# Squared-ReLU attention and feed-forward in one kernel: last keys transposed on their own, the centering mean from one sum, one batch's score bursts moved by a column

## Chip, cores, metric

One core of a Trainium2 chip. The metric is the device time of one execution in microseconds (us). The chip gives several executions of each kernel.

## The reference, cut to what matters

```python
# batch 8, heads 12, seq S = 448, head_dim 64, d_model 768, d_ff 3072
scores = scale * np.matmul(q, k.transpose(0, 1, 3, 2))
attn = np.maximum(scores, 0.0) ** 2 / S
x = np.matmul(attn, v)                       # then heads side by side: (8, 448, 768)
mu = np.mean(x, axis=-1, keepdims=True)
var = np.mean((x - mu) ** 2, axis=-1, keepdims=True)
xn = (x - mu) / np.sqrt(var + 1e-06) * g_ln
out = x + np.maximum(xn @ w_ch1, 0.0) @ w_ch2
```

## The kernel before

The order of work is written by hand. The first batch's attention runs alone (about 29 us). From then on the attention of batch b+1 is fed in "bursts" between the 24 columns of the first feed-forward layer of batch b. A column is 12 half-width matmuls and takes 1.13 us. A burst is three score tiles: TensorE makes scores, ScalarE and VectorE apply the ReLU, VectorE squares. Two heads make a pair; there are 48 pairs, six for each batch. The attn-V product of a pair ("attn-V" below) is put on TensorE at the start of a later burst. From the third batch on, q and k are transposed by DMA (`dma_start_transpose` on the SyncE queue); earlier ones by TensorE.

```python
def load_early():                       # first two heads: staged as fp32, cast on chip
    ...
    nc.sync.dma_start(k_st[:SS, :, NF], k[0, :2, SF:].rearrange("h s d -> s h d"))   # last 64 keys
    nc.vector.tensor_copy(first_q[0][:, :2], q_st.rearrange("p (h j d) -> p h j d", h=2, j=NJ))
    nc.scalar.copy(first_k[0][:, :2, :NF], k_st[:, :, :NF])
    nc.vector.tensor_copy(first_k[0][:SS, :2, NF], k_st[:SS, :, NF])
...
def av_out(i, ps, evac_by):             # eviction of attn-V, then what the centering needs
    ...
    if b == 0:
        if pr < GAIN_FIRST:             # GAIN_FIRST = 3: "gain multiplication"
            nc.vector.tensor_scalar(xc[:, pr, :], xT_of(b, pr), g_sb[:, pr:pr + 1], None, op0=Alu.mult)
    elif pr == 1:
        nc.vector.tensor_add(xs, xT_of(b, 0), xT_of(b, 1))
    elif 1 < pr < NPAIR - 1:            # running sum of the first five parts
        nc.vector.tensor_add(xs, xs, xT_of(b, pr))
...
def first():                            # the mean: ones times (sum of five), plus ones times the sixth
    for n, part in enumerate((xs, xT_of(b, K1 - 1))):
        for c in range(2):
            nc.tensor.matmul(mean_ps[c * D:(c + 1) * D, :], ones[:, :D], part,
                             start=(n == 0), stop=(n == 1))
...
def excursion(n, ...):                  # a burst
    if len(ready) > 1: ...              # attn-V of two pairs together
    elif ready and ready[0] % NPAIR == NPAIR - 2:
        next_AV(**how)                  # attn-V of pair 16 (batch 2), at batch 1's seventh burst
    took = [slots.pop(0) for _ in range(n)]
    for m, (i, t) in enumerate(took):
        att_QK(i, t, ...)
    for i, t in took:
        att_square(i, t)
...
STATS_AT = {0: (18, 21, 23), 1: (10, 16, 19, 22), 2: (2, 5, 8, 14)}
IN_REST = (1, 4, 7, 10, 13, 16, 19)
...
bursts = IN_FIRST if b == 0 else [n + (2 if b == 1 else 0) for n in IN_REST]   # b == 1: 3,6,9,12,15,18,21
```

## Time and profile before

| | before |
|---|---|
| executions | 521.97 (median), 521.89, 522.72 us |
| profiled execution | 522.75 us, span 521.0 us |
| TensorE busy | 513.3 us, 99% |
| first matmul of the feed-forward ("first weight matmul") | 29.03 us |

From part 1 of the page of before: engine, busy time (share of the span), instructions.

```profile
PE 513.3 (99%) x5705; PEld 311.5 (60%) x5705; DVE 367.6 (71%) x650; ACT 277.1 (53%) x456; POOL 222.5 (43%) x255
```

From the waits view of before, TensorE only: who waited for what, total us, times, longest. TensorE's only wait after the start-up:

```profile
PE sc L284 <- DMA qkT_t<-qk_ring: 1.0, 1, 1.0
```

From the timeline of before, batch 1's first layer. Columns: start, duration, engine, line, operation, out and in, count, and in brackets idle time before it and what ended it. SPq is the SyncE queue issuing DMAs; `qkT_t` is a transposed q/k tile, `at` an attention tile, `xc` the centred activations.

```profile
96.98 4.93 SPq L256 DMA_TRANSPOSE qkT_t<-qk_ring  x2
...
102.53 0.35 PE L284 MATMUL sc<-qkT_t 64*64 64x448 bf16 x2
...
103.87 0.38 PE L284 MATMUL sc<-qkT_t 64*64 64x448 bf16 x2 [0.99 <-DMA qkT_t<-qk_ring]
...
115.10 3.57 PE L429 MATMUL f<-xc,w 128*64 128x448 bf16 x36
...
116.82 1.69 DVE L302 TENSOR_TENSOR at<-at 128x896 bf16<-128x896 bf16 x3
...
118.51 0.92 PE L319 MATMUL f<-at,v_ring 128*64 128x448 bf16 x8
...
119.36 0.55 PE L289 MATMUL sc<-qkT_t 64*128 64x448 bf16 x4
```

Read it in two halves. The second half of the fourth burst's last-key scores (103.87 us) waits 0.99 us for a transpose that was issued at 96.98 us. Further down, the 36 matmuls after the sixth burst are three columns; VectorE's three squarings of that burst end at 116.82 + 1.69 = 118.51 us; the attn-V of pair 16 (8 matmuls, `at` as input) starts at the same time and the seventh burst's scores at 119.36 us.

From the chain that ended last, before (start, us, engine and line, count), at a mean:

```profile
196.07 0.38 PE f L388 x4
```

The four mean matmuls take 0.38 us: two half-width matmuls run side by side, so a pair costs 0.19 us.

From the timeline of before, the start-up (`xc<-xT,g_sb` is the gain multiplication; POOL rows are load issues of GpSimd):

```profile
1.23 3.46 PE L598 MATMUL f<-w,ones 128*128 128x256 bf16 x17 [1.23 <-DVE w L103]
...
6.91 0.92 ACT L299 ACTIVATE at<-sc 128x896 bf16<-128x896 f32 x1 [0.46 <-PE sc L289]
...
13.13 0.72 POOL L147 DMA_DIRECT2D w<-in_k_dram  x1
13.63 0.34 DVE L363 TENSOR_SCALAR xc<-xT,g_sb 128x448 bf16<-128x448 bf16 x1
...
29.03 0.73 PE L716 MATMUL f<-xc,w 128*128 128x448 bf16 x3
```

### The profile page before, as it was taken

The page shows a single profiled execution, that of the slowest core. Times are in us where ns is not written, and L with a number is a line of the kernel's source. Part 1 is how long each engine was busy: PE and PEld are TensorE (multiplying, and loading weights), DVE is VectorE, ACT ScalarE, POOL GpSimd, SP SyncE. Part 2 cuts the span into 40 slices and gives each one's busy share as a digit, 9 for nine tenths or more (in the row PEclk, how much of TensorE's full clock was granted, in tenths as well). Part 3 has the DMA queues.
Part 4 walks back from the last instruction along what each step waited for, and adds up shares of the span by engine and source line. Part 5 has one row for each costly group of instructions (what it writes and reads, how often), then busy time and mean ns, then how long its engine had stood idle before and what let it go on. Part 6 is the DMA issues. An engine that isn't in the chain of part 4 may idle for free.

```text
span 521.0 us, 13617 instructions
## 1 busy us (share of the span) xinstructions
PE 513.3 (99%) x5705; PEld 311.5 (60%) x5705; DVE 367.6 (71%) x650; ACT 277.1 (53%) x456; POOL 222.5 (43%) x255
## 2 busy tenths in 40 slices
PE   8999999999999999999999999999999999999996
PEld 4445566456765566655787556655666556665665
DVE  5966779778958669587685867787695866950255
ACT  6985643776247662476624766476524765234320
POOL 8727114788423853237632376237532000320031
PEclk9999999999999999999999999999999999999999
DMA  9999999999546992669924699369924300250022
GB/s 138 190 196 202 186 203 149 153 186 113 79 101 87 120 92 64 121 73 115 95 66 106 75 113 142 76 79 126 80 69 99 62 1 3 64 121 2 1 56 68
DMA packets 175261, 53.03 MB, mean 102 GB/s; under 512 B 154208, under 2 KB 175200, under 8 KB 175200
## 3 DMA queue, kind: packets, MB, share of 16 engines
q0 software_dynamic: 103552, 25.74, 53.8%
q1 hardware_dynamic: 71120, 26.06, 26.8%
q8 instruction: 44, 0.72, 0.6%
q10 hardware_dynamic: 528, 0.37, 0.2%
q14 instruction: 17, 0.14, 0.1%
HBM read 51.91 MB, written 11.01 MB: 121 GB/s over the span
## 4 chain that ended last, share of the span: by engine, by line
PE 92%; DVE 3%; DMA 2%; ACT 1%; POOL 0%; issue 0%; POOLq 0%
PE f L429 41%; PE f L497 34%; PE f L319 5%; PE sc L289 4%; PE f L480 3%; DVE at L302 2%; PE f L289 2%; DMA qkT_t<-qk_ring 1%; PE sc L284 1%; DMA w<-in_k_dram 1%; ACT at L299 1%; PE f L342 1%; PE f L716 1%; DVE xT L358 1%; DVE qkT_t L271 1%; PE f L388 1%
## 5 line engine op out<-in xcount | busy, mean ns | idle before, releaser
L429 PE MATMUL f<-xc,w 128*64 128x448 bf16 x2256 | 225.4, 353 | 0.1
L429 PEld LDWEIGHTS <-w 128*64 128x64 bf16 x2256 | 125.6, 110 | 91.7 <-issue 13.3
L431 ACT ACTIVATE h<-f 128x448 bf16<-128x448 f32 x188 | 102.7, 546 | 102.5 <-PE f L429 97.9
L497 PE MATMUL f<-w,s_sb 128*64 128x384 bf16 (+2 forms) x1584 | 130.1, 324 | 0.0
L497 PEld LDWEIGHTS <-s_sb 128*64 128x64 bf16 x1584 | 93.4, 110 | 33.9
L299 ACT ACTIVATE at<-sc 128x896 bf16<-128x896 f32 x120 | 103.2, 919 | 5.7 <-PE sc L289 4.6
L302 DVE TENSOR_TENSOR at<-at 128x896 bf16<-128x896 bf16 x168 | 95.4, 618 | 4.3 <-ACT at L299 4.1
L530 POOL TENSOR_TENSOR o_t<-o_t,x_tok 128x384 f32<-128x384 f32 x26 | 24.4, 937 | 153.0 <-ACT o_t L529 153.0
L169 POOL DMA_DIRECT2D qk_ring<-in_q_dram x36 | 47.1, 1308 | 85.0 <-DMA qkT_t<-qk_ring 59.7
L295 DVE TENSOR_SCALAR at<-f 128x448 bf16<-128x448 f32 x89 | 52.7, 619 | 30.7 <-PE f L289 30.7
L529 ACT ACTIVATE o_t<-f,rstd 128x384 f32<-128x384 f32 x26 | 15.1, 581 | 94.7 <-DVE acc_t L534 35.9
L491 DVE TENSOR_TENSOR s_sb<-h 128x1536 bf16<-128x1536 bf16 x65 | 64.1, 1002 | 0.0
L170 POOL DMA_DIRECT2D qk_ring<-in_k_dram x36 | 56.1, 1559 | 12.0 <-DMA w<-in_moe_w_ch_dram 12.0
L497 PE MATMUL f<-w,h 128*64 128x384 bf16 x624 | 52.9, 326 | 0.0
L171 POOL DMA_DIRECT2D qk_ring<-in_k_dram x36 | 47.7, 1325 | 5.2 <-DMA w<-in_moe_w_ch_dram 4.9
L497 PEld LDWEIGHTS <-h 128*64 128x64 bf16 x624 | 37.1, 110 | 14.0
L530 POOL TENSOR_TENSOR acc_t<-acc_t,x_tok 128x384 f32<-128x384 f32 x24 | 28.9, 1210 | 22.3 <-ACT acc_t L529 22.3
L319 PE MATMUL f<-at,v_ring 128*64 128x448 bf16 x288 | 35.9, 356 | 0.5 <-DVE xT L358 0.3
L181 POOL DMA_DIRECT2D v_ring<-in_v_dram x36 | 33.5, 1242 | 0.1
L395 DVE SCALAR_TENSOR_TENSOR xc<-f,g_sb,xc 128x448 bf16<-128x448 f32 x45 | 28.5, 677 | 6.7 <-PE f L388 6.0
L358 DVE TENSOR_SCALAR xT<-f 128x448 bf16<-128x448 f32 x33 | 20.3, 617 | 14.5 <-PE f L319 13.7
L289 PE MATMUL sc<-qkT_t 64*128 64x448 bf16 x192 | 30.0, 356 | 0.0
(87 smaller groups left out, 392.2 us busy)
## 6 DMA issues: line engine op xcount, KB each, us to landing
w<-in_moe_w_ch_dram POOLq DMA_DIRECT2D x6, 768.0 KB, 12.6
w<-in_moe_w_ch_dram POOLq DMA_DIRECT2D x4, 1152.0 KB, 29.3
v_ring<-in_v_dram POOLq DMA_DIRECT2D x21, 192.0 KB, 5.7
qk_ring<-in_q_dram POOLq DMA_DIRECT2D x36, 112.0 KB, 5.1
qk_ring<-in_k_dram POOLq DMA_DIRECT2D x36, 96.0 KB, 5.1
out_dram<-o_t SPq DMA_DIRECT2D x8, 168.0 KB, 2.2
out_dram<-acc_t SPq DMA_DIRECT2D x7, 168.0 KB, 2.2
out_dram<-o_t SPq DMA_DIRECT2D x8, 144.0 KB, 2.1
```

Source lines behind the costliest of these rows:

```text
L170: nc.gpsimd.dma_start(k_to[:, :NF], k[b, heads, :SF].rearrange("x (p t) d -> p t x d", t=NF))
L171: nc.gpsimd.dma_start(k_to[:SS, NF], k[b, 2 * a:2 * a + 2, SF:].rearrange("x s d -> s x d"))
L289: nc.tensor.matmul(by_j(half[hh]), k_of(i, r, t, P), q_of(i, r), start=True, stop=True)
L295: nc.vector.tensor_scalar(at[:, x], half[x], 0.0, None, op0=Alu.max)
L299: nc.scalar.activation(at, ps[:, :, :S], Act.Relu)
L302: nc.vector.tensor_mul(attn[i, t], attn[i, t], attn[i, t])
L319: nc.tensor.matmul(ps[hh * D:(hh + 1) * D, :], weights, values, start=start, stop=stop)
L429: nc.tensor.matmul(ps[c * D:(c + 1) * D, :], w1[:, ki, n0:n0 + D], xc[:, ki, :], start=(ki == 0), stop=(ki == K1 - 1))
L431: nc.scalar.activation(h[:, ni, CARRY:], ps, Act.Relu)
L491: nc.vector.tensor_tensor(s_sb[:, n], x, y, op=op)
L497: nc.tensor.matmul(ps[c * D:(c + 1) * D, :d1 - d0], stat[:, ki, c * D:(c + 1) * D], w2[:, slot, ki, d0:d1], start=(start and ki == 0), sto ...
L530: nc.gpsimd.tensor_tensor(o_t, o_t, x_half(m, dh), op=Alu.add)
```

## The change

Its intent: take two waits out of the start-up by loading and transposing the last 64 keys of the first two pairs separately; take a pair of matmuls out of each mean; and give batch 1's fourth burst one more column of time so that its transpose is there.

```diff
-        nc.sync.dma_start(k_st[:SS, :, NF], k[0, :2, SF:].rearrange("h s d -> s h d"))
-        nc.vector.tensor_copy(first_k[0][:SS, :2, NF], k_st[:SS, :, NF])
...
         if i == 0:
-            for t, cp in enumerate((nc.vector.tensor_copy, nc.scalar.copy)):
+            for t, cp, n in ((0, nc.vector.tensor_copy, S), (1, nc.scalar.copy, SF)):
                 ps = bf_view(next_f())
-                pe_T(0, t, ps)
-                c = slice(t * S, (t + 1) * S)
-                cp(flat(0)[:, c], ps[:, c])
+                pe_T(0, t, ps, range(NJ - t))
+                cp(flat(0)[:, t * S:t * S + n], ps[:, :n])
...                                                     # pair 1 likewise without its last keys
+    def first_last_keys():
+        ps = bf_view(next_f())
+        for i in range(2):
+            pe_T(i, 1, ps, [NF], i * SS)
+        for i in range(2):
+            nc.vector.tensor_copy(flat(i)[:, S + SF:2 * S], ps[:, i * SS:(i + 1) * SS])
...
-        elif 1 < pr < NPAIR - 1:
+        elif pr > 1:
             nc.vector.tensor_add(xs, xs, xT_of(b, pr))
...
-            for n, part in enumerate((xs, xT_of(b, K1 - 1))):
-                for c in range(2):
-                    nc.tensor.matmul(mean_ps[c * D:(c + 1) * D, :], ones[:, :D], part,
-                                     start=(n == 0), stop=(n == 1))
+            for c in range(2):
+                nc.tensor.matmul(mean_ps[c * D:(c + 1) * D, :], ones[:, :D], xs, start=True, stop=True)
...                                                     # step_fine(0), after the third score tile
-            warm_up(3)
+            first_last_keys()
+            warm_up(2)
...                                                     # end of the first batch's attention
+        mean_part(i - 2)
         att_T(i + 1, nc.scalar.copy, next_f())
-        mean_part(i - 2)
         mean_part(i - 1)
...
-    STATS_AT = {0: (18, 21, 23), 1: (10, 16, 19, 22), 2: (2, 5, 8, 14)}
+    STATS_AT = {0: (18, 21, 23), 1: (10, 14, 17, 22), 2: (2, 5, 8, 14)}
+    IN_SECOND = (3, 6, 9, 13, 16, 19, 21)
-            bursts = IN_FIRST if b == 0 else [n + (2 if b == 1 else 0) for n in IN_REST]
+            bursts = (IN_FIRST, IN_SECOND, IN_REST)[min(b, 2)]
-    SUMS_AT = (0, 1, 2, 4, 7, 13)
+    SUMS_AT = (0, 1, 2, 4, 7, 11)
...
-        load_heads(0, [("q", 2, 2), ("k", 2, 2), ("k last", 2, H - 2), ...
+        load_heads(0, [("q", 2, 2), ("k", 2, 2), ("k last", 0, H), ...
         att_T(0)
-        warm_up(5)
+        warm_up(3)
```

So of batch 1's bursts the fourth, fifth and sixth move from columns 12, 15, 18 to 13, 16, 19; the seventh stays at 21.

More of the change, by code (lines that the diff above doesn't have):

```diff
@@ L222, in by_j, with pe_T @@
         return x.rearrange("p (j s) -> p j s", j=NJ)
-    def pe_T(i, t, ps):
+    def pe_T(i, t, ps, tiles=range(NJ), c0=0):
         b, pr = divmod(i, NPAIR)
-        c0 = t * S
-        for j in range(NJ):
+        for j in tiles:
             rows = SP if t == 0 else P if j < NF else SS
@@ L268, in att_T @@
         ps = bf_view(bank)
-        for t in range(2):
-            pe_T(i, t, ps)
-        (copy or nc.vector.tensor_copy)(flat(i)[:, :2 * S], ps)
+        pe_T(i, 0, ps)
+        pe_T(i, 1, ps, range(NJ - (i == 1)), S)
+        n = S + (SF if i == 1 else S)
+        (copy or nc.vector.tensor_copy)(flat(i)[:, :n], ps[:, :n])
+    def first_last_keys():
[4 more added lines that the diff above has]
+            nc.vector.tensor_copy(flat(i)[:, S + SF:2 * S], ps[:, i * SS:(i + 1) * SS])
     def att_QK(i, t, relu_by=nc.scalar, between=None):
@@ L837 @@
     with tc.manual_schedule(engines=set(ENGINES)):
-        load_heads(0, [("q", 2, 2), ("k", 2, 2), ("k last", 2, H - 2), ("q", 4, 4), ("k", 4, 4), ("v", 0, 4),
+        load_heads(0, [("q", 2, 2), ("k", 2, 2), ("k last", 0, H), ("q", 4, 4), ("k", 4, 4), ("v", 0, 4),
                        ("v last", 0, H), ("q", 8, 4), ("k", 8, 4), ("v", 4, 4), ("v", 8, 4)])
```

## The prediction

> **What bounds the kernel now.** TensorE: 99% busy over the 521.0 us span (page, part 1), full granted clock in nearly every slice (part 2), 92% of the chain that ended last. The windows view shows it not full in 0 to 29 us (start-up attention, VectorE and ScalarE both 95-100% busy from 10 us), 102 to 104 us (busy 1.01 of 2.00), and the last 20 us. Elsewhere only less TensorE work helps.
>
> **What the change does, piece by piece.**
>
> 1. *Mean from one running sum.* Four half-width matmuls per batch become two. In the chain, products end at 196.07 us and the next start at 196.45, so the four cost 0.38 us and a pair 0.19 us: saved in each of batches 1 to 7. The added VectorE addition (0.39 us in the timeline) has slack and should cost nothing.
>
> 2. *Last keys on their own.* TensorE waited 0.33 us at 7.69 us for the last keys' load and 0.28 us at 5.66 us for their cast. The first relu should start near 6.4 us instead of 6.91. The gain is soon caught: the fourth score burst now waits for two copies queued behind the second squaring, the next keys land only at 10.5 us (transposes began at 10.34), the first values at 11.44, where attn-V already waits. I expect 0.1 to 0.2 us left at 29 us. The reordered mean is neutral: both orders wait for the same eviction.
>
> 3. *Batch 1's bursts.* The waits view gives one 0.99 us TensorE wait ending at 103.87 us, for a q/k transpose issued at 96.98 us that took 6.85 us. It hangs on the load queue, behind the last weight block (landed about 79.1 us), so I take 103.83 us as pinned. One more column (1.13 us) now runs before it. Being pinned, this swallows the earlier gains (about 0.35 us): altogether 1.13 us ahead here, not 0.99 + 0.35.
>  But the sixth burst moves from column 18 to 19 and the seventh stays at 21: two columns between them, not three. The seventh begins with attn-V of the pair whose last squaring ended at 118.51 us (timeline), 3.24 us after the sixth burst's matmuls (115.27). With three columns those matmuls need it at about 118.9; with two, at 117.75. The Trainium skill ("TensorE: Matmul & The Clock Gate", Part 3, The mechanism) says matmuls start and end in strict program order; this trace's in-order gap at 103 us agrees. About 0.8 us of stall there gives most of the 1.13 us back: net 0.3 us.
>
> **Sum.** 0.3 us through batch 1's first layer (pieces 2, 3 and batch 1's mean), plus 6 x 0.19 = 1.13 us for batches 2 to 7: about 1.5 us, all on TensorE's critical path.
>
> **Prediction: 520.5 us, range 519.3 to 521.5.** Faster by over 2%: 0.01; within 2%: 0.985; slower by over 2%: 0.005.
>
> **What would show each step.** (1) 14 mean matmuls instead of 28; each seven-product stage 0.19 us shorter. (2) First relu near 6.4 us; first weight matmul (29.03 us) at most 0.3 us earlier. (3) The wait at 103 us down to 0-0.2 us, the transpose still landing at about 103.8; a new TensorE wait of 0.5-0.9 us on VectorE's squaring near 118 us.
>
> **What would make it wrong.** Without the stall near 118 us the gain is 2.2-2.4 us (519.7). If start-up gains more and the transpose lands earlier, more. If loads shift later, or a later transpose (landing 113.4, needed 113.55) becomes a wait, it shrinks towards nothing. Before's three runs spread by 0.8 us, half the gain.

## The result, and the profile after

| | before | after |
|---|---|---|
| median | 522.05 us (4 runs, 521.89 to 522.72) | 522.01 us (4 runs, 521.47 to 522.27) |
| ratio, after to before | | 0.9996, 95% interval 0.9978 to 1.0013 |
| span of the profiled execution | 521.0 us | 520.2 us |

The forecast was 520.5 us with 519.3 to 521.5 around it. The time did not move.

Of the page after, part 1:

```profile
PE 512.8 (99%) x5688; PEld 310.4 (60%) x5688; DVE 370.8 (71%) x658; ACT 276.9 (53%) x456; POOL 222.7 (43%) x255
```

The waits view after, TensorE only. The wait on the transpose is gone; after the start-up there is now this one, twice:

```profile
PE f L323 <- DVE at L306: 0.4, 2, 0.3
```

The timeline after, batch 1's first layer (line numbers are a few higher than before):

```profile
94.72 5.71 SPq L253 DMA_TRANSPOSE qkT_t<-qk_ring  x2
...
104.42 0.36 PE L288 MATMUL sc<-qkT_t 64*64 64x448 bf16 x4
...
115.63 2.44 PE L431 MATMUL f<-xc,w 128*64 128x448 bf16 x24
...
117.35 1.69 DVE L306 TENSOR_TENSOR at<-at 128x896 bf16<-128x896 bf16 x3
...
117.90 0.36 PE L323 MATMUL f<-at,v_ring 128*64 128x448 bf16 x2
...
118.55 0.38 PE L323 MATMUL f<-at,v_ring 128*64 128x448 bf16 x2 [0.29 <-DVE at L306]
...
119.09 0.57 PE L323 MATMUL f<-at,v_ring 128*64 128x448 bf16 x4 [0.16 <-DVE at L306]
...
119.59 0.55 PE L293 MATMUL sc<-qkT_t 64*128 64x448 bf16 x4
```

The transpose was issued at 94.72 us, 2.26 us earlier than in the profile before. But an early issue is not an early landing. The DMA views of before and of after, narrowed to this one issue, give the time from issue to landing at their end:

```profile
qkT_t<-qk_ring SPq DMA_TRANSPOSE x1, 6.8
qkT_t<-qk_ring SPq DMA_TRANSPOSE x1, 9.4
```

The first is before's (issued at 96.98, landed at 103.83 us), the second after's (issued at 94.72, landed at 104.11 us). TensorE ran 0.5 us later in after, and the scores that need the transpose began at 104.43 us: here the extra column did cover a late landing. At column 12 the burst would have been held up in this execution too, by about 1.1 us (an estimate, worked out below). Near 118 us only two columns (24 matmuls) lie between the sixth burst and attn-V. The attn-V starts at 117.90 us, and its second and third parts wait for VectorE's squarings. From the rest of the sixth burst (115.63 us) to the seventh burst's scores is 3.96 us; before it was 4.26 us with one column more, so with 1.13 us taken off one would expect 3.13 us. The stall costs 0.83 us, although the brackets add up to only 0.29 + 0.16 us of idle time: a matmul that restarts after a wait counts as busy until its modelled end, and the next one no longer overlaps it (the eight of this attn-V take 0.92 us together in before, and two alone take 0.36 to 0.38 us here).

The chain after, at the same mean:

```profile
196.10 0.19 PE f L391 x2
```

0.19 us instead of 0.38, in each of batches 1 to 7.

The timeline after, start-up:

```profile
1.23 3.79 PE L600 MATMUL f<-w,ones 128*128 128x256 bf16 x17 [1.23 <-DVE w L103]
...
6.83 2.54 ACT L303 ACTIVATE at<-sc 128x896 bf16<-128x896 f32 x3 [0.46 <-PE sc L293]
...
9.13 0.28 DVE L275 COPY qkT_t<-f 128x64 bf16<-128x64 bf16 x2
...
9.37 0.47 PE L288 MATMUL sc<-qkT_t 64*64 64x448 bf16 x4 [0.57 <-ACT at L303]
...
13.38 0.79 POOL L150 DMA_DIRECT2D w<-in_k_dram  x1
...
13.69 0.58 DVE L367 TENSOR_SCALAR xc<-xT,g_sb 128x448 bf16<-128x448 bf16 x1
...
29.72 0.54 PE L719 MATMUL f<-xc,w 128*128 128x448 bf16 x2
```

The first relu starts at 6.83 instead of 6.91 us. The fourth score burst starts its first half (9.37 us) after the first copy of last keys, which ended at 9.32 us, and its second half after the second copy (9.13 + 0.28 = 9.41 us); before it was at 9.29 us. (The bracket names ScalarE, whose relu ended at the same moment, 9.37 us; the same coincidence is in keys_only and after_third, and in before the burst ran 0.68 us ahead of the end of that relu, so I read the copies as what it waits for.) Then the three gain multiplications take 0.58 (shown), 0.60 and 0.40 us in place of 0.34 to 0.36, and the first weight matmul is at 29.72 us, 0.69 us later than in the profile before.

Adding the two profiles up: +0.69 us (start), -0.19 us (batch 1's mean), -1.11 us (the wait at 103 us that before's execution had and that the extra column covered here), +0.83 us (stall), -1.13 us (six means): -0.91 us, and the last 27 us of products indeed start at 488.71 us after and 489.62 us before. But this sum contains two terms, the start and the wait, that may belong to these two executions and not to the kernels. The experiments ask that first.

### The profile page after: what moved, and what is told of

It is laid out like the page before. It is cut to its first block, busy times and chain, and to the rows that moved or that the text cites. A ratio compares the mean times of both kernels' runs of the same rounds, so it can differ in the third digit from the quotient of the medians.

```text
span 520.2 us, 13589 instructions
## 1 busy us (share of the span) xinstructions
PE 512.8 (99%) x5688; PEld 310.4 (60%) x5688; DVE 370.8 (71%) x658; ACT 276.9 (53%) x456; POOL 222.7 (43%) x255
## 4 chain that ended last, share of the span: by engine, by line
PE 93%; DVE 4%; ACT 2%; issue 0%
PE f L431 41%; PE f L499 34%; PE f L323 5%; PE sc L293 4%; PE f L482 3%; DVE at L306 2%; PE f L293 2%; ACT at L303 1%; PE sc L288 1%; PE f L346 1%; PE f L600 1%; PE f L719 1%; DVE xT L362 1%; PE f L229 1%; DVE qkT_t L268 1%; ACT h L433 0%
## 5 line engine op out<-in xcount | busy, mean ns | idle before, releaser
L170 POOL DMA_DIRECT2D qk_ring<-in_k_dram x36 | 55.0, 1528 | 12.6 <-DMA w<-in_moe_w_ch_dram 12.6
L171 POOL DMA_DIRECT2D qk_ring<-in_k_dram x36 | 46.6, 1294 | 6.4 <-DMA w<-in_moe_w_ch_dram 4.8
L532 POOL TENSOR_TENSOR acc_t<-acc_t,x_tok 128x384 f32<-128x384 f32 x24 | 28.8, 1209 | 22.3 <-ACT acc_t L531 19.6
```

What stands on the lines that cost most here:

```text
L170: nc.gpsimd.dma_start(k_to[:, :NF], k[b, heads, :SF].rearrange("x (p t) d -> p t x d", t=NF))
L171: nc.gpsimd.dma_start(k_to[:SS, NF], k[b, 2 * a:2 * a + 2, SF:].rearrange("x s d -> s x d"))
L532: nc.gpsimd.tensor_tensor(o_t, o_t, x_half(m, dh), op=Alu.add)
```

## The experiments

Theory A: the wait at 103 us belongs to some executions of before only, while the stall near 118 us is in every execution of after; the start gives nothing. Rival B: the wait is there in every execution of before, as predicted, and the start gives or costs a fixed amount.

Sixteen runs on four chips (five rounds each). All results were correct. "us" is the median with lowest and highest.

| kernel | us | ratio to before, 95% interval |
|---|---|---|
| before_again | 522.47 (521.76 to 524.57) | 1.0008, 0.9990 to 1.0026 |
| after_again | 521.93 (521.33 to 522.22) | 0.9992, 0.9980 to 1.0004 |
| mean_only | 522.02 (520.83 to 523.98) | 1.0000, 0.9980 to 1.0020 |
| bursts_only | 522.81 (522.30 to 525.05) | 1.0017, 1.0000 to 1.0033 |
| keys_only | 522.93 (522.38 to 523.99) | 1.0002, 0.9979 to 1.0025 |
| after_b5 | 521.12 (520.78 to 521.39) | 0.9969, 0.9948 to 0.9990 |
| mean_b5 | 521.30 (520.39 to 522.05) | 0.9972, 0.9949 to 0.9995 |
| after_psum | 522.14 (521.83 to 522.65) | 0.9989, 0.9968 to 1.0011 |
| b4_only | 522.21 (521.68 to 522.92) | 0.9991, 0.9977 to 1.0006 |
| mean_again | 520.52 (519.96 to 521.73) | 0.9961, 0.9945 to 0.9976 |
| mean_b5_again | 520.80 (519.95 to 521.60) | 0.9963, 0.9948 to 0.9979 |
| gain2 | 521.02 (520.45 to 522.26) | 0.9970, 0.9952 to 0.9987 |
| mean_third | 520.92 (520.22 to 523.89) | 0.9976, 0.9955 to 0.9997 |
| mean_bursts | 521.61 (520.88 to 522.92) | 0.9985, 0.9968 to 1.0003 |
| after_third | 521.35 (521.15 to 522.19) | 0.9979, 0.9964 to 0.9994 |
| after_order | 522.77 (521.30 to 523.01) | 0.9997, 0.9982 to 1.0013 |

Before itself, in the rounds of the four chips, had medians of 522.22, 522.49, 523.08 and 522.81 us and executions from 521.18 to 525.79 us. That spread is larger than any piece of the change, so the traces carry as much of the argument as the times. From each of the profiles I took the length of batch 1's first layer (its first matmul to the first matmul of the second layer). It does not contain the means, and nothing of the start-up:

| placing of bursts 4 to 7 | length in each profile, us |
|---|---|
| 12, 15, 18, 21 (before, before_again, mean_only, keys_only, mean_again, mean_third) | 39.08, 37.96, 40.41, 39.93, 38.28, 37.86 |
| 13, 16, 19, 21 (after, after_again, after_third, bursts_only, mean_bursts, after_psum) | 38.79, 38.79, 38.79, 38.79, 38.79, 38.81 |
| 13, 15, 18, 21 (after_b5, mean_b5, mean_b5_again, gain2, b4_only) | 37.97, 37.97, 39.08, 39.22, 37.96 |

This table is the core of the answer. The old placing takes 37.9 us when no transpose is late and up to 2.5 us more when some are. The change's placing takes 38.79 us in every one of six profiles (after_order, a seventh with another order of one product, comes below). It buys protection from late transposes and pays 0.83 us for it in every profiled execution. The third placing is as short as the first, to 0.1 us, when nothing is late.

What the protection is worth can be estimated from all eighteen profiles. At column 12 the fourth burst's last-key scores begin 18.52 us after the layer's first matmul (before: 102.53 - 84.01). The transpose that they need landed 17.6 to 20.2 us after that matmul, later than 18.52 us in fifteen of the eighteen. If the landing does not depend on the burst's column (not tested), a burst at column 12 would have been held up by nothing to 1.7 us, 0.7 us on average. That is an estimate; it stands against the 0.83 us of the stall.

### before_again: the same kernel, profiled once more

No edit.

> The kernel before, unchanged, profiled a second time. Theory A (the 0.99 us TensorE wait ending at 103.87 us was an accident of the first profile, whose execution took 522.75 us, the longest of four): the wait is gone or under 0.3 us, the transpose is issued about 2 us earlier (near 94.7 us, as in the profile after), the run is near 522.0 us and its span near 520.2. Theory B (the wait is pinned, as predicted): 0.8 to 1.1 us of wait again, transpose issued near 97 us. Ratio 1.000 under both.

Measured: timeline, SyncE queue alone:

```profile
95.14 4.85 SPq L256 DMA_TRANSPOSE qkT_t<-qk_ring  x2
```

The transpose is issued at 95.14 us, not 96.98, and the fourth burst's wait is nearly gone: its four last-key matmuls take 0.61 us in place of 0.36, too little for the waits view. So the size of the wait is not a property of the kernel: theory A on this point. But the earlier issue is not the reason. The transpose took 8.4 us to land and did so at 103.53 us, only 0.30 us before the first profile's; it was TensorE that came to the burst 0.81 us later, and so found its data there. (The prediction took the landing of one profile as "pinned". Over the eighteen profiles it came at 101.2 to 105.6 us, 6.4 to 9.4 us after an issue at 94.4 to 98.2 us. It is not independent of TensorE either: it came last, at 105.60 us, in bursts_only, whose layer started last, at 86.53 us, and first, at 101.22 us, in mean_bursts, whose layer started among the first, at 83.59 us.) The run was no faster, because its start was slow: the first weight matmul came at 29.84 us. Two lines of its timeline show why; a gain multiplication of 1.00 us ends 0.10 us after the end of the GpSimd load issue that it overlaps (20.24 + 1.08 = 21.32):

```profile
20.24 1.08 POOL L152 DMA_DIRECT2D s_sb<-in_v_dram  x1
20.42 1.00 DVE L363 TENSOR_SCALAR xc<-xT,g_sb 128x448 bf16<-128x448 bf16 x1
```

### after_again

No edit.

> The kernel after, unchanged, profiled a second time. Theory A: first weight matmul again near 29.7 us (0.7 later than before's 29.03), the three gain multiplications on VectorE again 0.4 to 0.6 us instead of 0.34, and the seventh burst again about 0.8 us late; ratio to before 0.998 to 1.001. Theory B (start-up loss was noise, bursts gain): first weight matmul near 28.9 to 29.1, ratio 0.997 or less.

Measured: ratio 0.9992; the stall and both its waits again, within 0.01 us. But the first weight matmul came at 29.15 us and the three multiplications took 0.34 us each. So theory A was wrong to expect a fixed loss in the start: the 0.69 us of the first comparison was chance. B, which expected 0.997 or less, is not borne out.

### mean_only, mean_again, mean_third: the mean alone

The edit is the `av_out` and `first` part of the change.

> Before with only the mean taken from one running sum. Both theories: 7 x 0.19 = 1.33 us less, ratio near 0.9975; 14 mean matmuls instead of 28. If the added VectorE addition cost anything, the gain is smaller and a new wait on VectorE shows.

> Before with only the mean from one sum, a second time, since its first times (520.8 to 524.0) were too wide to say anything. By its trace each batch from 2 to 7 is 0.19 us shorter: 1.13 us that no wait can swallow, and 0.19 us of batch 1 that a pinned wait may. Ratio 0.9970 to 0.9982 if the late transposes are no commoner than in before; if it is 0.999 or more, the waits in batch 1 are commoner or longer with TensorE ahead.

> Before with only the mean from one sum, on the same chip as the next two. Ratio to before 0.9960 to 0.9978.

Measured: 1.0000, then 0.9961, then 0.9976: a first miss, then more than expected, then as expected. In every trace the mean is 0.19 us instead of 0.38, and no new wait on VectorE follows. The first profile, of an execution of 523.77 us, shows what spoilt it, in the waits view for batch 1's layer:

```profile
PE sc L284 <- DMA qkT_t<-qk_ring: 1.5, 2, 1.3
PE sc L289 <- DMA qkT_t<-qk_ring: 0.5, 1, 0.5
```

Three late transposes, at the first, fourth and sixth burst, made that layer 40.41 us long. The other two profiles (520.53 and 520.22 us) had none. With the executions this wide, 1.33 us is just what three times five rounds can show.

### bursts_only

```diff
-    STATS_AT = {0: (18, 21, 23), 1: (10, 16, 19, 22), 2: (2, 5, 8, 14)}
+    STATS_AT = {0: (18, 21, 23), 1: (10, 14, 17, 22), 2: (2, 5, 8, 14)}
+    IN_SECOND = (3, 6, 9, 13, 16, 19, 21)
-            bursts = IN_FIRST if b == 0 else [n + (2 if b == 1 else 0) for n in IN_REST]
+            bursts = (IN_FIRST, IN_SECOND, IN_REST)[min(b, 2)]
-    SUMS_AT = (0, 1, 2, 4, 7, 13)
+    SUMS_AT = (0, 1, 2, 4, 7, 11)
```

> Before with only batch 1's columns moved (bursts, statistics, weight sums). Theory A: no wait at 103 us was there to take away in most executions, and the seventh burst stalls 0.8 us near 118 us on VectorE's squaring: about 0.8 us slower, ratio near 1.0015. Theory B: about 0.3 us faster, ratio near 0.9994.

Measured: 1.0017 (1.0000 to 1.0033), 0.9 us slower with an interval from nothing to 1.7 us, as theory A says and against B; without the execution of 525.05 us it is 0.5 us. The layer is 38.79 us. The profiled execution (525.05 us, the worst of the six) had an unlucky start: k and v came late, TensorE idled, and its granted clock fell, in the windows view (stretch, length, busy time and count, clock, DMA, GB/s):

```profile
10.00:20.00 10.00, 8.68 (x87) 0.83 1.44 150
```

Its first weight matmul was at 31.55 us. This kernel's start is before's, so the start-up lottery is not new with the change.

### keys_only

The edit is the start of the change, without the moved `mean_part`.

> Before with only the first two pairs' last keys loaded and transposed on their own (bursts, mean and the mean's place in the order as before). Theory A (the head start is caught within 12 us by the copies, loads and VectorE, and what is left is decided by how long three VectorE multiplications are held up by load issues on GpSimd): first weight matmul anywhere in 29.0 to 30.2 us like before's three ordinary profiles (29.03, 29.84, 30.10), first relu near 6.83; ratio 0.999 to 1.0005. Rival B (the piece gives a real head start): first weight matmul under 28.9, ratio 0.999 or less.

Measured: 1.0002; first weight matmul at 29.31 us, first relu no earlier than in after (6.89 us). Rival B falls by the trace; the interval of the times (0.9979 to 1.0025) would still allow its 0.999. Its batch 1 layer had the late transposes of the old placing, in the waits view (1.08 and 0.40 us):

```profile
PE sc L288 <- DMA qkT_t<-qk_ring: 1.5, 2, 1.1
```

Over all profiles the first weight matmul came at 28.77 to 31.55 us in ten profiles with the old start (median 29.04) and at 29.09 to 30.11 us in six with the new one (median 29.5; after_psum and gain2, which change the multiplications themselves, are not counted). No head start is left. The sum behind those numbers is close: from the first eviction of attn-V to the first weight matmul takes 16.03 us, plus whatever the three multiplications took above 3 x 0.34 us. For instance mean_third 29.00 - 12.83 = 16.17 with multiplications of 0.34, 0.48 and 0.34; keys_only 29.31 - 13.10 = 16.21 with 0.52, 0.34, 0.34; before_again 29.84 - 13.06 = 16.78 with 0.39, 0.38, 1.00. All come back to 16.03 (only bursts_only, whose clock fell, does not). Kernels with the moved `mean_part` come to 16.12 (after 29.72 - 13.04 = 16.68 with 0.58, 0.60, 0.40; after_again 29.15 - 13.03 = 16.12 with 0.34 each). So the new order of the mean costs 0.09 us.

### after_psum: the multiplication from another memory

```diff
-                nc.vector.tensor_scalar(xc[:, pr, :], xT_of(b, pr), g_sb[:, pr:pr + 1], None, op0=Alu.mult)
+                nc.vector.tensor_scalar(xc[:, pr, :], ps, c2, g_sb[:, pr:pr + 1], op0=Alu.mult, op1=Alu.mult)
```

> After, with the three gain multiplications on VectorE reading the PSUM bank instead of the SBUF copy of the same values. If the long ones (0.58, 0.60, 1.00 us against 0.34) are held up by GpSimd's load issues[...], all three now take 0.60 to 0.64 us whatever GpSimd issues, and never 0.7 or more; none ends 0.1 us after the end of a load issue except by chance. If VectorE is slow there for another reason, they vary still. Time near after's, within 0.3 us.

Measured, VectorE's timeline:

```profile
13.32 0.67 DVE L367 TENSOR_SCALAR xc<-f,g_sb 128x448 bf16<-128x448 f32 x1
...
16.58 0.68 DVE L367 TENSOR_SCALAR xc<-f,g_sb 128x448 bf16<-128x448 f32 x1
...
20.37 0.68 DVE L367 TENSOR_SCALAR xc<-f,g_sb 128x448 bf16<-128x448 f32 x1
```

Always the same, as expected, though 0.67 us and not 0.60 to 0.64. Reading from SBUF, the multiplication takes 0.34 us, or longer; all 27 profiled ones that took over 0.35 us end 0.07 to 0.11 us after the end of a GpSimd load issue. The three reads from PSUM do not test the rule by themselves, since every issue that began before one of them had ended before it did. The evictions of attn-V (`xT<-f`), which read PSUM too, do: 32 of them began under an issue that was still running, or within 0.06 us of its end, when they ended, and they took 0.61 to 0.62 us, like the others. In after, for one, an eviction runs from 20.16 to 20.77 us under an issue that lasts from 20.08 to 21.11 us. The Trainium skill ("SBUF — State Buffer", section "Who interferes with whom") states the rule: VectorE and GpSimd share a pair of SBUF ports, a `tensor_scalar` in a two-port mode takes it, and whoever comes second is blocked until the first is done. These traces agree, but for the eight multiplications named at the end of this document; the case for GpSimd as the blocker rests on the matching end times, not on an experiment that moved GpSimd's issues. As a fix it is worth nothing: the run was no faster.

### after_b5: three columns before the seventh burst again

```diff
-    IN_SECOND = (3, 6, 9, 13, 16, 19, 21)
+    IN_SECOND = (3, 6, 9, 13, 15, 18, 21)
-    STATS_AT = {0: (18, 21, 23), 1: (10, 14, 17, 22), 2: (2, 5, 8, 14)}
+    STATS_AT = {0: (18, 21, 23), 1: (10, 16, 19, 22), 2: (2, 5, 8, 14)}
```

> After, with batch 1's fifth and sixth bursts put back at columns 15 and 18 (and statistics as before), the fourth staying at 13: three columns again before the seventh. Theory A: the two waits on VectorE's squaring near 118 us vanish, 5.62 us between sixth and seventh burst, batch 1's stage 0.83 us shorter than after's where no transpose is late, so about 521.1 us, ratio near 0.9975; a late transpose may be waited for at the sixth burst. Rival: if the stall was not the cause of the 0.83 us, the time stays near 521.9.

Measured: 521.12 us, as expected to 0.02 us, ratio 0.9969. TensorE's timeline, three columns and then attn-V without a wait:

```profile
114.83 3.57 PE L431 MATMUL f<-xc,w 128*64 128x448 bf16 x36
118.23 0.92 PE L323 MATMUL f<-at,v_ring 128*64 128x448 bf16 x8
119.09 0.55 PE L293 MATMUL sc<-qkT_t 64*128 64x448 bf16 x4
```

114.83 to 119.09 us is 4.26 us for three columns, as in before. The layer is 37.97 us, 0.82 us shorter than after's. This shows that the stall was what cost it. (The statistics moved back with the bursts and were not tested apart, but the 0.83 us lie wholly between the sixth and the seventh burst.) The times say the same: in the same rounds after_psum, which is after but for the three multiplications, took 521.83 to 522.65 us, and after_b5 520.78 to 521.39 us.

### mean_b5, mean_b5_again, b4_only: the fourth burst alone

`IN_SECOND = (3, 6, 9, 13, 15, 18, 21)` on before's start, with and without the new mean. The last weight sum moves to column 11, as in after.

> Before's start, with the mean from one sum and the fourth burst at column 13, fifth to seventh at 15, 18, 21. Theory A: 7 x 0.19 = 1.33 us less, no stall at the seventh burst, the wait at 103 us mostly covered: lowest time near 520.3, ratio near 0.9970. Rival B (the new start is worth something): slower than the run with the new start by more than 0.3 us.

> The better version (mean from one sum, fourth burst alone at 13, before's start) a second time on another chip: ratio 0.9960 to 0.9980, no wait on a transpose or a squaring in batch 1.

> Before with only batch 1's fourth burst moved, from column 12 to 13 (fifth to seventh stay at 15, 18, 21; the last weight sum moves from 13 to 11), so that it takes the wait at 103 us away without making the stall near 118. Theory A (the wait is there in some executions only, worth 0.3 to 0.5 us on average): ratio 0.9985 to 0.9995, no wait on a transpose at the fourth burst. Rival (the wait is there in nearly every execution, about 1 us): ratio near 0.9978. Rival (never there outside profiles): 1.0000.

Measured: 0.9972 and 0.9963 with the mean, 0.9991 (0.9977 to 1.0006) without it. The last is the nearest thing to a price of the wait alone: 0.5 us faster, with an interval from 1.2 us faster to 0.3 us slower, so the times alone exclude neither of its rivals. Against the expectation for mean_b5_again, its profile had a wait of 0.75 us on a transpose, at the sixth burst, which sits at column 18 again; gain2, with the same placing, 0.89 us. That is what the change's move of the sixth burst to 19 guards against. The prediction named this danger but put it on the wrong side: of eleven profiles with the sixth burst at column 18, five show such a delay (0.3 to 1.6 us), and of seven with it at 19, one (after_order, 0.54 us).

### gain2: one multiplication fewer

`GAIN_FIRST = 2` on mean_b5.

> The better version with two instead of three gain multiplications in the start-up (the third part goes through the addition and ScalarE's scaling as parts 3 to 5 do). It drops the multiplication near 20.4 us, that took 0.34 to 1.01 us. First weight matmul 0.3 to 1.0 us earlier than the usual 29.1 to 30.1, less about 0.2 us given back between the second and third part; ratio to the better version 0.9990 to 1.0000. If the second part's scaling on ScalarE waits for its two copies, nothing is won.

Measured: first weight matmul at 28.60 us, about 0.3 us less than the sum above gives for its first eviction, and batch 0's first layer, which follows, took 39.22 instead of 39.00 us. 0.1 us is left, nothing that a time could show: 0.9970 against 0.9963 for mean_b5_again in the same rounds.

### mean_bursts and after_third: the chain of steps on one chip

mean_bursts is mean_third plus the moved columns; after_third is mean_bursts plus the new start and the new order.

> mean_third plus batch 1's moved columns as in after (13, 16, 19, 21), with before's start. Theory A (stall 0.83 us, the removed wait worth 0 to 0.5 us on average): 0.3 to 0.9 us slower than mean_third. Theory B (as predicted: net gain of 0.3 us or more): faster than mean_third. In the trace 5.32 us from sixth to seventh burst and the two waits on the squaring near 118 us in both.

> The kernel after, unchanged: mean_bursts plus the new start and the mean's new place in the order. Theory A (no head start left, 0.09 us lost by the order): within 0.4 us of mean_bursts. As predicted (0.1 to 0.2 us gained): indistinguishable from that by time, but the trace decides: from the first eviction of attn-V to the first weight matmul 16.12 us plus what the multiplications took over 1.02 us in all, against 16.03 in kernels with the old order.

Measured, medians of the same rounds: before 522.81, mean_third 520.92, mean_bursts 521.61, after_third 521.35 us. The mean gives, the bursts take 0.7 us back (0.3 us by the means of the same runs), the start does nothing that could be told from 0.3 us. The intervals overlap; it is the agreement with the 38.79 us in each trace, and with bursts_only, that carries this. On this chip after was faster than before by 0.2% (0.9964 to 0.9994), more than in the first comparison.

### after_order: is it the last squaring?

```diff
-        order = [NF, 0, 1, 2] if i % 2 else [0, 1, 2, NF]
+        order = [NF, 0, 1, 2] if i % 2 else [0, 1, 2, NF] if half is not None or i < NPAIR else [0, NF, 1, 2]
```

> After, with attn-V of even pairs from 12 on taken in the order first keys, last keys, second, third instead of last keys at the end. If the stall is the wait for the last of three squarings (third keys), the last keys' two matmuls now run before it: 5.13 us from sixth to seventh burst instead of 5.32, other stages as in after; 0.2 us less in all.

Measured: the total missed its expectation (ratio 0.9997). The start was slow (first weight matmul 30.11 us), and late transposes delayed the fourth burst by 0.31 us and the sixth by 0.54 us. The fourth burst's transpose was issued at 98.15 us, later than in any other profile, and landed at 105.06 us, so column 13 is no full protection either. The distance from the start of the sixth burst was therefore 5.67 us and not 5.13. Measured from the end of that burst's scores, TensorE's timelines of after_order,

```profile
116.29 0.76 PE L323 MATMUL f<-at,v_ring 128*64 128x448 bf16 x6
...
120.33 0.38 PE L323 MATMUL f<-at,v_ring 128*64 128x448 bf16 x2 [0.15 <-DVE at L306]
120.64 0.55 PE L293 MATMUL sc<-qkT_t 64*128 64x448 bf16 x4
```

and of after_third in the same rounds,

```profile
114.41 0.76 PE L323 MATMUL f<-at,v_ring 128*64 128x448 bf16 x6
...
117.92 0.38 PE L323 MATMUL f<-at,v_ring 128*64 128x448 bf16 x2 [0.29 <-DVE at L306]
118.45 0.57 PE L323 MATMUL f<-at,v_ring 128*64 128x448 bf16 x4 [0.15 <-DVE at L306]
118.95 0.55 PE L293 MATMUL sc<-qkT_t 64*128 64x448 bf16 x4
```

give 120.64 - 116.29 = 4.35 us against 118.95 - 114.41 = 4.54 us. That is 0.19 us less: two matmuls no longer stand behind the wait. So it is the last squaring that is waited for.

## Why the prediction was wrong

- **Mean: right.** 14 matmuls in place of 28, 0.19 us for each of seven batches, 1.33 us in all, and the added VectorE addition costs nothing.
- **Start: wrong in size, right in mechanism.** The head start is caught at the fourth score burst, as argued. But it began smaller (relu at 6.83, not 6.4 us): TensorE's transposes waited for the warm-up matmuls, 17 of which took 3.46 us in the first profile and 3.79 in the second and in before_again. The Trainium skill ("TensorE: Matmul & The Clock Gate", Part 1) says that the point at which the clock is released varies from run to run. The traces agree in that the first matmuls are slow and then become faster, from 0.42 to 0.27 us each for the warm-up ones, at about 4.2 us in before, 4.9 in after_third and 5.9 in after; in after_third the first relu came at 6.48 us, near the predicted 6.4. The views give a granted clock of 1.00 over the whole stretch, so that it is the clock is not shown. What was to be left at 29 us, 0.1 to 0.2 us, is not there: keys_only 1.0002. The reordered mean was called neutral and costs 0.09 us. None of the start's larger swings (28.8 to 31.6 us) comes from the change.
- **Stall near 118 us: right.** 0.8 us was predicted, 0.83 us measured, on the squaring named. The columns behind the wait did not go ahead: no later matmul started in the two gaps.
- **The wait at 103 us: this is the step that failed.** The prediction said "I take 103.83 us as pinned" and counted 1.13 us of gain there, so that the stall would leave "net 0.3 us". The landing is not pinned: over eighteen profiles it came at 101.2 to 105.6 us, and TensorE came to the burst at varying times too. What column 12 loses by it is therefore not 1.13 us each time but, by the estimate above, nothing to 1.7 us and 0.7 us on average; b4_only's times put it at 0.5 us. Of the six profiles with the old placing, three lost 1.1 to 2.5 us to late transposes in this layer, one lost 0.3 us and two next to nothing. The profile I read was of one of the slower executions, 0.8 us above two of the other three, and I made its wait a property of the kernel. The stall of 0.83 us, in contrast, is there each time. In place of a net gain of 0.3 us, the timed comparisons give a loss: 0.9 us (interval from nothing to 1.7) in bursts_only, and 0.3 us by means or 0.7 us by medians between mean_third and mean_bursts.
- **Sum.** -1.33 (mean) + 0.3 to 0.9 (bursts) + 0.1 (order) is -0.3 to -0.9 us; the three comparisons of the change gave ratios of 0.9996, 0.9992 and 0.9979, that is -0.2, -0.4 and -1.1 us. The forecast was -1.5.

Open: how often transposes are late in executions that are not profiled. The six profiles of the old placing would put the average wait near 1 us (mean length 38.92 against about 37.9 us), which would make the moved bursts break even; the estimate from all eighteen, 0.7 us against a stall of 0.83 us, comes to nearly the same, and the timed runs to a loss of 0.3 to 0.9 us. These agree within their spread: the moved bursts gain nothing, and how much they lose is not settled. Why the loads, and with them the transposes, vary by more than 3 us was not tried.

Versions that came out ahead of before: the new mean alone (0.9961 and 0.9976, but 1.0000 in a third run), or with the fourth burst at 13 and the others left (0.9963 and 0.9972); after_b5 (0.9969) had the narrowest spread of these, 0.6 us. Against after itself, in the same rounds, only mean_third was run (520.92 against 521.35 us, with overlapping executions).

## What to carry to other kernels

Before you count a wait as removable, profile the unchanged kernel twice, above all if the profiled execution is slower than the rest: here one wait of 1 us, read from one trace, was half of the gains counted (1.13 of about 2.3 us). Compare landings and not issues: a transpose issued 2.26 us earlier landed 0.28 us later. Moving a stage later to hide a late load shortens the time to the next stage that depends on it, and that cost is paid in every execution, while the lateness of the load varies. An idle bracket understates a stall on a pipelined engine (0.45 us shown, 0.83 us lost), so measure stalls by the distance between two fixed points.

## What the Trainium skill lacked or had wrong

- "SBUF — State Buffer", "Who interferes with whom", describes the block between VectorE and GpSimd, but not what it does to a short operation: a multiplication of 0.34 us took up to 1.01 us, ending 0.07 to 0.11 us after the load issue. It says that the first to issue holds the ports for its whole instruction; here eight multiplications that began 0.04 to 0.09 us after a load issue (in after_order 17.13 against 17.04 us) still took 0.34 us, while those that were held up had begun 0.18 us or more after it. The spans recorded on GpSimd are rough, so this may be the record and not the ports.
- No page says how far a DMA transpose behind a loaded queue varies between executions of one program: issued at 94.4 to 98.2 us here, landing 6.4 to 9.4 us later, at 101.2 to 105.6 us.
- No page gives what a wait inside a stream of half-width matmuls costs beyond its idle time: 0.83 us for 0.45 us.
